# Half-row matmul units in the second output segment, 13 upper matmuls for 14, refitted bank estimate, new written orders

## The chip, the cores and the metric

One core of a Trainium2 chip runs the kernel. The metric is the device time of one execution in microseconds (us). The kernel runs in float32; its matmuls read float32r, most of them as high and low parts whose products are added up.

## The reference

The input `x` has 2048 rows of 576. Two attentions with 32 heads of width 18 are computed from it, A with keys and values of its own for each head, B with one key and one value head shared by all, and mixed by a gate:

```python
g = sigmoid((x * gate_w).sum(-1, keepdims=True))
q, k, v = split(x @ wqkv)                      # A: 32 heads of 18
a = merge(softmax(q @ k.T * 18**-0.5) @ v) @ A_wo
q, k, v = x @ B_wq, x @ B_wk, x @ B_wv         # B: k and v shared by the heads
b = merge(softmax(q @ k.T * 18**-0.5) @ v) @ B_wo
return g * a + (1 - g) * b
```

`B_wq` and `B_wk` are scaled by 8, so scores are large, and the row maximum is taken off before the exponential.

## The kernel before, in words

**Units of work.** There are 64 heads (`NU`), B's 32 first, then A's 32. A head has 16 steps (blocks of 128 keys), so there are 1024 steps, counted by `T`. A step has four banks of scores (128 keys by 512 queries each): an `s` in the written orders is one such matmul (line 674), followed by an exponential on ACT from the bank into a `pt` tile (line 682). 22 steps (`LEAD`) ahead, the maxima are made by matmuls of queries by keys (line 629): an `m` is one with a reduction on DVE (line 638); an `x` and a `y` work together, ACT taking the positive part of a difference (line 632) that DVE then joins and reduces (line 635). The sums over keys (line 689) put `pt` times values into one fixed bank, `acc`; a number in an order, 1 to 7, says how many quarters (128 columns each) of such sums follow.

**TensorE in halves.** `s` uses partitions 0 to 63 (`SB`), the maxima partitions 64 to 127 (`MB`), and the two run side by side in the two row halves of the array. The sums use all 128 rows in four column blocks. So the orders collect `s` and `m` into groups, and put the sums between the groups.

**Units.** Projections of A's values (32 units), of the later query and key rows (42), and the output projection (segments of the 1152 rows, 32 units each) are put in between. A unit is 14 (`PROJ`) or 12 matmuls into one bank of 288 to 296 columns. A whole unit, `U` (`whole_unit`, line 864), uses all 128 rows and leaves by one copy on ACT or one addition on DVE. A half unit (`half_step`, line 873) is split by rows: its upper halves, `A`, run in the half of the maxima into one bank, its lower halves, `B`, in the half of the scores into a second bank. The upper bank leaves by ACT, the lower by an addition on DVE; where the destination holds a sum already, the upper one goes through the tile `tmp`, which POOL adds. In `PROJ`'s last two entries rows 64 to 127 of the weights repeat the rows 512 to 575 of the weight matrix, and the same rows of `x` hold its low part.

**Stages.** One written order is emitted per eight steps ("a run" of it): `PLAIN` without units; `HALF14` with one half unit of 14 (steps 18 to 273 for the values, 282 to 617 for the rows); `HALF12` with one half unit of the first output segment (steps 634 to 889); `DENSE` with four whole units of the second segment (steps 946 to 1001). The last 22 steps have an order of their own and four more whole units, and the third, short segment ends the kernel.

**Banks.** Seven PSUM banks besides `acc` take everything. Which bank a matmul gets is settled when the program is written: `Clock` follows TensorE, ACT and DVE with estimated durations (lines 33 to 36), and `first` picks the bank that should be free earliest. It sets no time by itself, but a matmul whose bank is still being read waits, and TensorE runs in order.

**The rest.** `slow` is a list of generators that move on once per two steps, first in, first out: the gates, `prep_wo` (loads output weights through the tile `wost`, splits them on POOL) and `normalise` (scales a finished tile of heads on POOL). `when(T, f)` calls `f` at step `T`. All loads are issued on SP's queue in program order; POOL issues the stores of what it has made.

Of the kernel before, what the change touches and what calls it, by code (L numbers as in the profile page):

```python
# [29 lines left out]
PROJ = [(a, b, k, 128) for a, b in (("h", "h"), ("l", "h"), ("h", "l")) for k in range(NKT - 1)] + \  # L30
       [("h", "h", NKT - 1, 128), ("l", "h", NKT - 1, 128)]

PITCH_S, STREAM, HALF_MM, LOAD, GAP = 228, 214, 120, 107, 14
TO_SUMS, FROM_SUMS, QUARTER = 113, 111, 214
EXP_T, EXP_D, RED_T, RED_D, TO_ACT, TO_DVE, FREED = 477, 605, 600, 681, 459, 432, 52
COPY_T, ADD_T, MAXED, COPIED = 370, 372, 180, 400


class Unit:
    def __init__(self, ops, n, dst, done, view=lambda f: f, how="copy"):  # L40
        self.ops, self.n, self.dst, self.done, self.view, self.how = ops, n, dst, done, view, how
        self.left, self.fp = {"a": 0, "b": 0}, {}


class Clock:


    def __init__(self):
        self.free = [0.0] * 7
        self.t = self.act = self.dve = self.last = 0.0  # L50
        self.mode, self.begun, self.tail = "", [0.0, 0.0], [0.0, 0.0]
        self.turns, self.count, self.held, self.diffs = {"s": 0, "m": 0}, 0, {}, []

    def turn(self, which):
        n = self.turns[which]
# [19 lines left out]
        k = min(range(7), key=lambda i: self.free[i])  # L75
        return k, self.free[k]

    def leave(self, k, s, act, pitch, lasts):
        if act:
            at = max(s + TO_ACT, self.act)  # L80
            self.act = at + pitch
        else:
            at = max(s + TO_DVE, self.dve)
            self.dve = at + pitch
        self.free[k] = at + lasts + FREED

    def bank(self, what, tile):
        k, free = self.first()
        if what in "smxy":
            s = self.matmul(tile, free, STREAM)  # L90
            act = what in "sx"
            if what == "y" and self.diffs:
                self.dve = max(self.dve, self.diffs.pop(0))
            self.leave(k, s, act, EXP_T if act else RED_T, EXP_D if act else RED_D)
            if what == "x":
                self.diffs.append(self.free[k])
        else:
            if self.mode == "s":
                self.t = max(self.tail)
            s = max(self.t, free) + (LOAD + 14 * (HALF_MM + 11) if what != "t" else STREAM)  # L100
            self.t, self.mode = s + 99, ""
            self.leave(k, s - STREAM, what == "U", COPY_T, COPY_T + 90)
        return k

    def open(self, part, tile):
# [7 lines left out]

    def close(self, part):
        k, s = self.held.pop(part)
        self.leave(k, s + HALF_MM - STREAM, part == "a", COPY_T if part == "a" else ADD_T, 90 + ADD_T)

    def sums(self, n):
        if self.mode != "p":
            self.t += TO_SUMS if self.mode == "s" else 0  # L120
            self.mode = "p"
        self.t += QUARTER * n

    def dve_extra(self, t):
        self.dve = max(self.dve, self.t) + t


def q_row(u):
# [8 lines left out]
def gated_mix_kernel(ctx: ExitStack, tc: tile.TileContext, xT, wall, wv, wo, out):  # L137
    nc = tc.nc
    P = 128
# [361 lines left out]
    def row_units():  # L501

        pool = L["px"]
        XR, WR = [], []

        def cut(c):
            return slice(292 * c, 292 * c + 292 if c < 6 else S)

        def load_wr(mt):
            WR.append(pool.tile([P, NKT, P], F32, name="wrst"))  # L510
            load5(WR[-1], wall[mt])

        def load_xr(c):
            XR.append(pool.tile([P, 2 * NKT - 1, 296], F32R, name="xr", bufs=2))
            n = 296 if c == 6 else 292
            dma(XR[-1][:, :, 0:n], x_d[:, :, cut(c)])

        def next_w(mt):
            W = {y: pool.tile([P, NKT, P], F32R, name=f"wr{y}") for y in "hl"}
            split(WR.pop(0), W["h"], W["l"], nc.gpsimd, nc.gpsimd)  # L520
            if mt + 1 < MT:
                load_wr(mt + 1)
            return W

        def both(st, n):
            hl = pool.tile([P, 2, 296], F32R, name="rhl", bufs=1)
            split(st, hl[:, 0, 0:n], hl[:, 1, 0:n], nc.gpsimd, nc.gpsimd)
            return hl[:, :, 0:n]

        load_wr(NT)  # L530
        load_xr(0)
        W = {NT: next_w(NT)}
        yield
        for mt in range(NT, MT):
            rs = slice(mt * P, (mt + 1) * P)
            first = pool.tile([P, 4, 292], F32, name="rst", bufs=1).rearrange("p c f -> p (c f)")
            for c in range(7):
                x = XR.pop(0)
                if (mt, c) != (MT - 1, 6):
                    load_xr((c + 1) % 7)  # L540
                n = 296 if c == 6 else 292
                b = (0, 292, 584, 876, 512, 0, 808)[c]

                def done(mt=mt, c=c, n=n, b=b, first=first, rs=rs):
                    dma(qk_d[:, rs, cut(c)].rearrange("a p f -> p a f"), both(first[:, b:b + n], n), nc.gpsimd)
                    if c == 3:
                        nc.gpsimd.tensor_tensor(first[:, 0:512], first[:, 512:1024], first[:, 0:512],
                                                op=OP.subtract)
                    if 3 <= c < 5:
                        cs = slice(256 * (c - 3), 256 * (c - 2))  # L550
                        d = both(first[:, cs], 256)
                        dma(kd_d[rs, 0:2, cs], d, nc.gpsimd)
                        dma(kd_d[rs, 2, cs], d[:, 0, :], nc.gpsimd)
                    if c == 6 and mt + 1 < MT:
                        W[mt + 1] = next_w(mt + 1)

                w = W[mt]
                yield Unit([(w[a][:, k, :], x[:, k if b_ == "h" else NKT + k, 0:n]) for a, b_, k, _ in PROJ],
                           n, first[:, b:b + n], done)

    def value_units():

# [25 lines left out]
        for st_ in range(16):  # L588
            if st_ < 15:
                load(st_ + 1)  # L590
            x = XV.pop(st_)
            for hf in range(2):
                yield Unit([(x[:, k if b == "h" else NKT + k, :], w[hf][a][:, k, :]) for a, b, k, _ in PROJ],
                           288, vst[hf][:, :, 0:18],
                           lambda st_=st_, hf=hf: dma(v_d[st_, :, 304 * hf:304 * hf + 304],
                                                      vst[hf].rearrange("p h d -> p (h d)")),
                           lambda f: f.rearrange("p (h d) -> p h d", d=18))

    VG = {}

# [39 lines left out]
    def max_rows(u):  # L640


        m = ms[u % 2]
        clk.dve_extra(MAXED)
        nc.vector.tensor_reduce(m[:, 0:16], MX.pop(u), axis=AX.X, op=OP.max, negate=True)
        mt = lead.tile([P, 32], F32, name="mt")
        nc.vector.transpose(mt, m)  # L647
# [63 lines left out]
    def head_out(u):  # L711
        oe = L["work"].tile([P, 512], F32, name="oe", bufs=1)
        nc.vector.tensor_copy(oe, acc)
        clk.dve_extra(COPIED)
        sums = lambda: dma(sum_d[u].rearrange("(j f) -> j f", j=4), oe[18:128:32, :])
        if u == NU - 2:
            sums()
# [19 lines left out]
    def normalise(t, at_end=False):  # L737
# [13 lines left out]
        g = P if t >= 7 else 32  # L751
        for c in range(0, P, g):
            nc.vector.reciprocal(sm[:n, c:c + g], sm[:n, c:c + g])  # L753
            yield
        (nc.vector if at_end else nc.gpsimd).tensor_tensor(sm[:n, :], sm[:n, :], gt[:n, :], op=OP.mult)
        dma(r_d[u0:u1, :].rearrange("h (s f) -> (h s) f", f=P), sm[:n, :])
# [93 lines left out]
    def tmp_row(tag="ol", bufs=1):  # L850
        return L["work"].tile([P, 288], F32, name="tmp", tag=tag, bufs=bufs)
# [21 lines left out]
    def half_step(op):  # L873
# [8 lines left out]
            u.fp[op] = bank_tile(clk.open(op, b == MB))  # L882
        else:
            clk.more(op, b == MB)
        x, y = u.ops[n]
        nc.tensor.matmul(u.fp[op][:, 0:u.n], x[b:b + 64], y[b:b + 64], start=(n == 0), stop=(n == len(u.ops) - 1))  # L886
        u.left[op] = n + 1
        if n + 1 < len(u.ops):
            return
        HALF[op].pop(0)  # L890
        clk.close(op)
        if op == "a":
            if u.how == "copy":
                leave_unit(u, u.fp["a"], "copy")
            else:
                u.tmp = tmp_row("half", 1)
                nc.scalar.activation(u.tmp, u.fp["a"][:, 0:u.n], AF.Copy)
        else:
            leave_unit(u, u.fp["b"], "add")
# [62 lines left out]
    def when(T, f):  # L962
        at.setdefault(T, []).append(f)
# [25 lines left out]
    for t0, rows, Ta, Tb in SEG:  # L989
        when(Ta, lambda t0=t0, rows=rows: slow.append(prep_wo(t0, rows)))  # L990
        when(Tb, lambda t0=t0, rows=rows: begin_units(out_proj(t0, rows, first=t0 == 0)))
    when(950, lambda: slow.append(prep_wo(8, [P])))
    when(980, load_gates)

    def keep_busy():
# [46 lines left out]


    PLAIN = "mssmsm 4 smsmsm 3 smmssx 3 smmsys 3 mssxysm 3 msxmssm 3 mssysms 3 msssmys 4 msmsms 3 smxssm 3"
    HALF14 = "ysmssm 4 xsmsms 4 sysmms 4 sAmsAsAsm 3 msAsmBBAABsAABABmsABABmsABABmBBAxBBBx 1 smsysm 4 yssmsm 2 msms 2 msmsms 4 sxsmms 4"
    HALF12 = "mssmsx 4 mssmsm 4 smssyms 4 msmssm 4 msmssm 4 sysmms 3 mssAAmBAAsAABsAABmBsAABmBBABAxBBmBBysxs 3 smsysm 3 smsmxs 3"
    DENSE = "smsysm 4 smsmsmUsmsx 4 smsysm 4 smsmsmUsmsx 4 smsysm 4 smsmsmUsmsx 4 smsysm 4 smsmsmUsmsx 4"
    plain = [(M, c) for p in range((LEAD + 2) // 2, NSTEP // 2)
             for M, c in [(2 * p, 2), (2 * p, 3)] + [(2 * p + 1, c) for c in range(4)]]

# [131 lines left out]
```

## Time and profile before

| | us |
|---|---|
| median of 3 runs | 2680.01 (2679.63 to 2680.86) |
| profiled execution, its own time | 2681.64 |
| profiled execution, span of the instructions | 2679.9 |
| PE / DVE / ACT / POOL busy in it | 2668.6 / 2422.7 / 2413.3 / 425.0 |

The busy time of PE comes from modelled ends of pipelined matmuls, so a full PE row means that matmuls follow each other, not that the array is filled. In the rows of the trace a line of the code stands with its engine, its operation, and output and inputs; "xN" after a merged row counts instructions, and a bracket tells how long the engine was idle before it, and what ended that. Row groups give the busy time, the mean length of one in ns and the idle time before them.

### The profile page before, as it was taken

The page shows a single profiled execution, that of the slowest core. Times are in us where ns is not written, and L with a number is a line of the kernel's source. Part 1 is how long each engine was busy: PE and PEld are TensorE (multiplying, and loading weights), DVE is VectorE, ACT ScalarE, POOL GpSimd, SP SyncE. Part 2 cuts the span into 40 slices and gives each one's busy share as a digit, 9 for nine tenths or more (in the row PEclk, how much of TensorE's full clock was granted, in tenths as well). Part 3 has the DMA queues.
Part 4 walks back from the last instruction along what each step waited for, and adds up shares of the span by engine and source line. Part 5 has one row for each costly group of instructions (what it writes and reads, how often), then busy time and mean ns, then how long its engine had stood idle before and what let it go on. Part 6 is the DMA issues. An engine that isn't in the chain of part 4 may idle for free.

```text
span 2679.9 us, 61494 instructions
## 1 busy us (share of the span) xinstructions
PE 2668.6 (100%) x23032; PEld 1353.3 (51%) x23032; DVE 2422.7 (90%) x4559; ACT 2413.3 (90%) x4787; POOL 425.0 (16%) x633
## 2 busy tenths in 40 slices
PE   9999999999999999999999999999999999999998
PEld 7645454444445445454454444545454454555545
DVE  4899999999999999999999999999999999998873
ACT  4399999999999999999999999999999999998776
POOL 2810000110003212322232112000200020111002
PEclk9999999999999999999999999999999999999999
DMA  8821112321224435444455454223321332233312
GB/s 278 329 89 60 49 44 62 83 68 50 60 57 143 132 112 148 135 147 132 148 183 163 142 157 152 78 75 90 107 72 54 103 102 63 73 99 112 106 36 90
DMA packets 190127, 293.68 MB, mean 110 GB/s; under 512 B 54738, under 2 KB 149282, under 8 KB 178252
## 3 DMA queue, kind: packets, MB, share of 16 engines
q1 hardware_dynamic: 170564, 224.02, 28.7%
q0 software_dynamic: 18368, 64.50, 6.5%
q8 instruction: 181, 2.97, 0.5%
q10 hardware_dynamic: 896, 1.23, 0.1%
q14 instruction: 118, 0.97, 0.1%
HBM read 203.29 MB, written 77.62 MB: 105 GB/s over the span
## 4 chain that ended last, share of the span: by engine, by line
PE 99%; DVE 0%; DMA 0%; issue 0%; SPq 0%; ACT 0%; DVEq 0%
PE acc L689 38%; PE bank L629 26%; PE bank L674 21%; PE bank L886 7%; PE bank L255 4%; PE bank L867 3%; PE acc L701 1%; DMA wst<-wall 0%; DVE mx L638 0%; DVE oacc L862 0%; PE bank L935 0%; PE bank L302 0%; DVE rl L925 0%; SPq L143 0%; DVE sm L753 0%
## 5 line engine op out<-in xcount | busy, mean ns | idle before, releaser
L682 ACT ACTIVATE pt<-bank 128x512 f32<-128x512 f32 x4096 | 2134.7, 618 | 154.3 <-PE bank L674 72.8
L638 DVE TENSOR_REDUCE mx<-bank 128x1 f32<-128x512 f32 x3096 | 1966.4, 683 | 127.4 <-PE bank L674 60.2
L674 PE MATMUL bank<-qs,ksb 56*128 56x512 f32 x2688 | 898.6, 429 | 1.5 <-issue 1.5
L629 PE MATMUL bank<-ksb,qs 54*128 54x512 f32 x2364 | 801.5, 423 | 0.1
L674 PEld LDWEIGHTS bank<-qs,ksb 56*128 56x128 f32 x2688 | 438.2, 184 | 258.6 <-DVE mx L638 125.6
L689 PE MATMUL acc<-pt,vb 128*19 128x512 f32 (+3 forms) x5240 | 565.8, 506 | 0.0
L689 PE MATMUL acc<-pt,vg 128*19 128x512 f32 (+3 forms) x5464 | 538.4, 481 | 0.0
L629 PEld LDWEIGHTS bank<-ksb,qs 54*128 54x128 f32 x2364 | 389.4, 184 | 276.2 <-ACT pt L682 129.0
L674 PE MATMUL bank<-qs,ksa 56*128 56x512 f32 x1408 | 460.7, 433 | 0.6 <-DVE ksb L219 0.5
L629 PE MATMUL bank<-ksa,qs 54*128 54x512 f32 x1232 | 426.8, 429 | 0.0
L635 DVE CUSTOM_DVE_ANT_0 junk<-bank,xb 128x512 bf16<-128x512 f32 x500 | 342.2, 684 | 31.1 <-PE bank L629 26.0
L632 ACT ACTIVATE xb<-bank 128x512 f32<-128x512 f32 x500 | 301.3, 628 | 12.0 <-PE bank L674 11.8
L674 PEld LDWEIGHTS bank<-qs,ksa 56*128 56x128 f32 x1408 | 222.7, 184 | 151.7 <-ACT pt L682 83.6
L629 PEld LDWEIGHTS bank<-ksa,qs 54*128 54x128 f32 x1232 | 203.7, 184 | 141.9 <-ACT pt L682 82.5
L217 POOL CAST mh<-mt 128x32 fp32r<-128x32 f32 x64 | 13.5, 210 | 1389.3 <-DVE mt L647 1389.3
L689 PEld LDWEIGHTS acc<-pt,vg 128*19 128x19 f32 x5464 | 103.3, 97 | 185.2 <-issue 163.2
L689 PEld LDWEIGHTS acc<-pt,vb 128*19 128x19 f32 x5240 | 90.3, 97 | 189.3 <-issue 176.3
L629 PE MATMUL bank<-kdb,qs 54*128 54x512 f32 x372 | 150.9, 434 | 0.0
L886 PE MATMUL bank<-xr,wrh 64*128 64x292 f32 (+1 forms) x756 | 145.7, 300 | 0.0
L886 PEld LDWEIGHTS bank<-xr,wrh 64*128 64x128 f32 x756 | 124.6, 186 | 0.0
L886 PE MATMUL bank<-vwh,xv 64*128 64x288 f32 x576 | 109.5, 299 | 0.0
L217 POOL CAST rhl<-rst 128x292 fp32r<-128x292 f32 (+2 forms) x54 | 22.6, 418 | 474.2 <-DVE rst L862 436.0
(142 smaller groups left out, 1959.7 us busy)
## 6 DMA issues: line engine op xcount, KB each, us to landing
qs<-qk SPq DMA_DIRECT2D x384, 144.0 KB
xr<-x_d SPq DMA_DIRECT2D x36, 1314.0 KB
ksa<-qk SPq DMA_DIRECT2D x132, 144.0 KB
qk<-phl POOLq DMA_DIRECT2D x32, 512.0 KB, 5.8
qk<-rhl POOLq DMA_DIRECT2D x36, 292.0 KB, 3.4
ksb<-qk SPq DMA_DIRECT2D x66, 144.0 KB
xv<-x_d SPq DMA_DIRECT2D x16, 576.0 KB
onh<-oh POOLq DMA_DIRECT2D x32, 256.0 KB, 3.5
```

The costliest lines, as they stand in the source:

```text
L217: eng_h.tensor_copy(h, src)
L255: nc.tensor.matmul(fp[:, p0:p0 + g], w[a][:kr, k, :], X[b][:kr, k, x0 + p0:x0 + p0 + g], start=(n == 0), stop=(n == len(PROJ) - 1))
L629: nc.tensor.matmul(pm, qs[u % 3][b:b + 54, i * P:(i + 1) * P], k, start=True, stop=True)
L632: nc.scalar.activation(MX["x", u, i], pm, AF.Relu)
L635: nc.vector.tensor_tensor_reduce(junk, pm, MX.pop(("x", u, i)), 1.0, -3e38, op0=OP.add, op1=OP.max, accum_out=MX[u][:, i, c:c + 1])
L638: nc.vector.tensor_reduce(MX[u][:, i, c:c + 1], pm, axis=AX.X, op=OP.max)
L674: nc.tensor.matmul(ps, kst(u)[b:b + 56, i * P:(i + 1) * P], qs[u % 3][b:b + 56, c * 512:(c + 1) * 512], start=True, stop=True)
L682: nc.scalar.activation(pt, ps, AF.Exp, scale=SCALE)
L689: nc.tensor.matmul(acc[32 * j:32 * j + 19, a:b], v_of(u, i), PT[u, i, j][:, a:b], start=(i == 0), stop=(i == 15), skip_group_check=True)
L701: nc.tensor.matmul(acc[32 * j:32 * j + 19, 256 * half + a:256 * half + b], v_of(NU - 1, i), pt[:, x + a:x + b], start=(i == 0), stop=(i == ...
L867: nc.tensor.matmul(fp[:, 0:u.n], x, y, start=(n == 0), stop=(n == len(u.ops) - 1))
L886: nc.tensor.matmul(u.fp[op][:, 0:u.n], x[b:b + 64], y[b:b + 64], start=(n == 0), stop=(n == len(u.ops) - 1))
```

## The change

It does six things. The durations of `Clock` are set anew, and it follows a few more events (the copy that a DVE addition waits for, the copy of `acc` that the next sums wait for, reciprocals). A `Unit` can have fewer upper matmuls, and the value and row units have 13 for 14: the last upper one multiplies the low part of the weights by the low part of `x`, a term that is left out elsewhere too. `HALF14` and `HALF12` have other orders. `DENSE` has half units for whole ones, four per eight steps as before. The tile `tmp` of half units shares its place with `wost`. The weights of the third segment are loaded from step 908 on instead of 950.

```diff
-PITCH_S, STREAM, HALF_MM, LOAD, GAP = 228, 214, 120, 107, 14
-TO_SUMS, FROM_SUMS, QUARTER = 113, 111, 214
-EXP_T, EXP_D, RED_T, RED_D, TO_ACT, TO_DVE, FREED = 477, 605, 600, 681, 459, 432, 52
-COPY_T, ADD_T, MAXED, COPIED = 370, 372, 180, 400
+STREAM, HALF_MM, LOAD, GAP = 214, 120, 107, 18
+LEAVE, TO_SUMS, FROM_SUMS, QUARTER = 98, 15, 116, 213.4
+EXP_T, EXP_D, RED_T, RED_D, JOIN_T, TO_ACT, TO_DVE, FREED = 482, 607, 600, 682, 616, 424, 425, 52
+COPY_T, ADD_T, MAXED, COPIED = 370, 372, 430, 605
...
-    def __init__(self, ops, n, dst, done, view=lambda f: f, how="copy"):
+    def __init__(self, ops, n, dst, done, view=lambda f: f, how="copy", upper=None):
         self.ops, self.n, self.dst, self.done, self.view, self.how = ops, n, dst, done, view, how
+        self.half = {"a": ops[:upper], "b": ops}
...
     def close(self, part):
         k, s = self.held.pop(part)
-        self.leave(k, s + HALF_MM - STREAM, part == "a", COPY_T if part == "a" else ADD_T, 90 + ADD_T)
+        s += HALF_MM - STREAM
+        if part == "a":
+            end = self.on_act(s, COPY_T) + COPY_T + 55
+            self.copies.append(end + 55)
+        else:
+            self.dve = max(self.dve, self.copies.pop(0))
+            end = self.on_dve(s, ADD_T) + ADD_T + 85
+        self.free[k] = end + FREED
 
     def sums(self, n):
+        if self.mode == "s":
+            self.t = max(self.tail) + LEAVE
         if self.mode != "p":
-            self.t += TO_SUMS if self.mode == "s" else 0
+            self.t += TO_SUMS
             self.mode = "p"
-        self.t += QUARTER * n
+        self.t = max(self.t, self.cleared) + QUARTER * n
...
# row_units and value_units: the Unit gets
+                           ..., upper=-1)
...
# half_step
-        x, y = u.ops[n]
-        nc.tensor.matmul(u.fp[op][:, 0:u.n], x[b:b + 64], y[b:b + 64], start=(n == 0), stop=(n == len(u.ops) - 1))
+        last = len(u.half[op]) - 1
+        x, y = u.half[op][n]
+        nc.tensor.matmul(u.fp[op][:, 0:u.n], x[b:b + 64], y[b:b + 64], start=(n == 0), stop=(n == last))
...
-                u.tmp = tmp_row("half", 1)
+                u.tmp = L["pool"].tile([P, 288], F32, name="tmp", tag="wost")
...
-    when(950, lambda: slow.append(prep_wo(8, [P])))
+    when(908, lambda: slow.append(prep_wo(8, [P])))
...
-    HALF14 = "ysmssm 4 xsmsms 4 sysmms 4 sAmsAsAsm 3 msAsmBBAABsAABABmsABABmsABABmBBAxBBBx 1 smsysm 4 yssmsm 2 msms 2 msmsms 4 sxsmms 4"
-    HALF12 = "mssmsx 4 mssmsm 4 smssyms 4 msmssm 4 msmssm 4 sysmms 3 mssAAmBAAsAABsAABmBsAABmBBABAxBBmBBysxs 3 smsysm 3 smsmxs 3"
-    DENSE = "smsysm 4 smsmsmUsmsx 4 smsysm 4 smsmsmUsmsx 4 smsysm 4 smsmsmUsmsx 4 smsysm 4 smsmsmUsmsx 4"
+    HALF14 = "ysmssm 4 mssmsm 3 smsmsm 3 xsmssm 4 msmssm 3 msAsABABAyBsABAABAsmBABsAABmBABABmBsxmBBxs 3 smmssm 4 mssymss 4 ysxssm 4"
+    HALF12 = "msmsms 4 smmsms 2 ysms 3 smmssx 4 mssmsm 3 smsy 2 sxmsms 3 smsmsm 4 smmsAsAABBAABBmBAsABmBsAAABABByBAsxBsm 3 yssxsm 4"
+    DENSE = "msABsmBABAsAABABmBBxBAsABAABsAABmBms 4 smsmsm 5 ABAsmsABABAsyBABABABxBsAmBABsAABmB 5 msysms 7 AsmsyBBABAsAABABmBAsABmBBAAsmBABABxs 3 smsmsy 4 smABABAsmBABsAAsAmBBABmBABABBAAsmBxs 4"
```

More of the change, by code (lines that the diff above doesn't have):

```diff
@@ L51, in __init__ @@
         self.mode, self.begun, self.tail = "", [0.0, 0.0], [0.0, 0.0]
-        self.turns, self.count, self.held, self.diffs = {"s": 0, "m": 0}, 0, {}, []
+        self.turns, self.count, self.held, self.diffs, self.copies = {"s": 0, "m": 0}, 0, {}, [], []
+        self.cleared = 0.0
     def turn(self, which):
@@ L76, in first, with on_act, on_dve @@
         return k, self.free[k]
[L78 to L85, printed above, removed]
+    def on_act(self, ready, pitch):
+        at = max(ready + TO_ACT, self.act)
+        self.act = at + pitch
+        return at
+    def on_dve(self, ready, pitch):
+        at = max(ready + TO_DVE, self.dve)
+        self.dve = at + pitch
+        return at
     def bank(self, what, tile):
@@ L90, in bank @@
             s = self.matmul(tile, free, STREAM)
[L91 to L96, printed above, removed]
-        else:
-            if self.mode == "s":
-                self.t = max(self.tail)
+            if what in "sx":
+                end = self.on_act(s, EXP_T) + EXP_D
+                if what == "x":
+                    self.diffs.append(end + 60)
+            else:
+                if what == "y" and self.diffs:
+                    self.dve = max(self.dve, self.diffs.pop(0))
+                end = self.on_dve(s, RED_T if what == "m" else JOIN_T) + RED_D
+        else:
+            self.t = (max(self.tail) + LEAVE if self.mode == "s" else self.t)
             s = max(self.t, free) + (LOAD + 14 * (HALF_MM + 11) if what != "t" else STREAM)
-            self.t, self.mode = s + 99, ""
-            self.leave(k, s - STREAM, what == "U", COPY_T, COPY_T + 90)
+            self.t, self.mode = s + LEAVE, ""
+            end = (self.on_act if what == "U" else self.on_dve)(s - STREAM, COPY_T) + COPY_T + 90
+        self.free[k] = end + FREED
         return k
@@ L115, in close, with other @@
         k, s = self.held.pop(part)
-        self.leave(k, s + HALF_MM - STREAM, part == "a", COPY_T if part == "a" else ADD_T, 90 + ADD_T)
+        s += HALF_MM - STREAM
+        if part == "a":
+            end = self.on_act(s, COPY_T) + COPY_T + 55
+            self.copies.append(end + 55)
+        else:
+            self.dve = max(self.dve, self.copies.pop(0))
+            end = self.on_dve(s, ADD_T) + ADD_T + 85
+        self.free[k] = end + FREED
     def sums(self, n):
+        if self.mode == "s":
+            self.t = max(self.tail) + LEAVE
         if self.mode != "p":
-            self.t += TO_SUMS if self.mode == "s" else 0
+            self.t += TO_SUMS
             self.mode = "p"
-        self.t += QUARTER * n
-    def dve_extra(self, t):
-        self.dve = max(self.dve, self.t) + t
+        self.t = max(self.t, self.cleared) + QUARTER * n
+    def other(self, pitch, acc=False):
+        self.dve = max(self.dve, self.t) + pitch
+        if acc:
+            self.cleared = self.dve + 100
 def q_row(u):
@@ L558, in row_units @@
                 yield Unit([(w[a][:, k, :], x[:, k if b_ == "h" else NKT + k, 0:n]) for a, b_, k, _ in PROJ],
-                           n, first[:, b:b + n], done)
+                           n, first[:, b:b + n], done, upper=-1)
     def value_units():
@@ L596, in value_units @@
                                                       vst[hf].rearrange("p h d -> p (h d)")),
-                           lambda f: f.rearrange("p (h d) -> p h d", d=18))
+                           lambda f: f.rearrange("p (h d) -> p h d", d=18), upper=-1)
     VG = {}
@@ L643, in max_rows @@
         m = ms[u % 2]
-        clk.dve_extra(MAXED)
+        clk.other(MAXED)
         nc.vector.tensor_reduce(m[:, 0:16], MX.pop(u), axis=AX.X, op=OP.max, negate=True)
@@ L713, in head_out @@
         nc.vector.tensor_copy(oe, acc)
-        clk.dve_extra(COPIED)
+        clk.other(COPIED, True)
         sums = lambda: dma(sum_d[u].rearrange("(j f) -> j f", j=4), oe[18:128:32, :])
@@ L753, in normalise @@
             nc.vector.reciprocal(sm[:n, c:c + g], sm[:n, c:c + g])
+            clk.other(110 + 6.5 * g)
             yield
@@ L884, in half_step @@
             clk.more(op, b == MB)
-        x, y = u.ops[n]
-        nc.tensor.matmul(u.fp[op][:, 0:u.n], x[b:b + 64], y[b:b + 64], start=(n == 0), stop=(n == len(u.ops) - 1))
+        last = len(u.half[op]) - 1
+        x, y = u.half[op][n]
+        nc.tensor.matmul(u.fp[op][:, 0:u.n], x[b:b + 64], y[b:b + 64], start=(n == 0), stop=(n == last))
         u.left[op] = n + 1
-        if n + 1 < len(u.ops):
+        if n < last:
             return
```

## The prediction

> **What bounds the kernel now.** The order of reading: the page's busy line and chain, then the stretches by stage, then the order of time on TensorE in one group of each kind.
>
> ```profile
> span 2679.9 us, 61494 instructions
> PE 2668.6 (100%) x23032; PEld 1353.3 (51%) x23032; DVE 2422.7 (90%) x4559; ACT 2413.3 (90%) x4787; POOL 425.0 (16%) x633
> PE 99%; DVE 0%; DMA 0%; issue 0%; SPq 0%; ACT 0%; DVEq 0%
> ```
>
> The chain that ended last lies on PE for 99% of the span. DVE and ACT, which empty the PSUM banks, are busy 90%. So it is PE's own order that sets the time, and what the change takes out of that order comes off the end, unless banks then come free too late.
>
> ```profile
> core 0: us, PE busy (x) PEld busy (x) DVE busy (x) ACT busy (x) POOL busy (x), PEclk, DMA share, GB/s
> 174.09:802.49 628.40, 628.40 (x5510) 303.39 (x5506) 589.11 (x1113) 592.14 (x1185) 26.57 (x55) 1.00 0.20 59
> 821.01:1645.83 824.82, 824.82 (x7230) 400.15 (x7226) 773.67 (x1462) 777.53 (x1555) 201.73 (x303) 1.00 0.48 146
> 1682.89:2305.23 622.34, 622.34 (x5637) 310.55 (x5634) 588.49 (x1113) 594.36 (x1185) 48.42 (x81) 1.00 0.29 83
> 2305.23:2435.76 130.53, 130.43 (x1293) 65.48 (x1289) 125.13 (x237) 126.92 (x253) 22.90 (x31) 1.00 0.33 98
> 2435.76:2609.62 173.86, 173.86 (x1235) 88.72 (x1231) 141.44 (x265) 132.61 (x253) 7.68 (x13) 1.00 0.26 79
> ```
>
> These stretches begin and end at first scores matmuls of the written orders: 32 and 42 runs of HALF14, 32 of HALF12, 7 of PLAIN, 7 of DENSE. One run (eight steps) takes 628.40/32 = 19.64 us and 824.82/42 = 19.64 in HALF14, 622.34/32 = 19.45 in HALF12, 130.53/7 = 18.65 in PLAIN, 173.86/7 = 24.84 in DENSE. The granted clock is 1.00 in all of them.
>
> Now PE in DENSE, in order of time (start, length):
>
> ```profile
> 2437.65 0.50 PE L674 MATMUL bank<-qs,ksa 56*128 56x512 f32 x1
> ...
> 2437.99 0.39 PE L674 MATMUL bank<-qs,ksa 56*128 56x512 f32 x1
> ...
> 2438.22 0.39 PE L674 MATMUL bank<-qs,ksa 56*128 56x512 f32 x1
> ...
> 2438.55 0.79 PE L867 MATMUL bank<-woh,oih 128*128 128x288 f32 x4
> ...
> 2440.99 1.05 PE L689 MATMUL acc<-pt,vg 128*19 128x512 f32 x8
> 2441.98 0.50 PE L674 MATMUL bank<-qs,ksa 56*128 56x512 f32 x1
> ...
> 2442.88 1.05 PE L689 MATMUL acc<-pt,vg 128*19 128x512 f32 x8
> 2443.87 0.50 PE L674 MATMUL bank<-qs,ksa 56*128 56x512 f32 x1
> ```
>
> A plain group (three scores and three maxima in the two row halves, then four quarters of sums) goes from 2441.98 to 2443.87: 0.90 to the sums, 0.99 for them. A pair costs 0.23 (2437.99 to 2438.22; in the sums below 0.228, the 214 + 14 ns of the kernel's own constants). The group with a whole unit goes from 2437.65 to 2441.98, 4.33 us; five pairs without a unit would take 0.90 + 2 x 0.23 + 0.99 = 2.35. So a whole unit costs 1.98 us, though 12 matmuls at the 0.134 of the next rows make 1.61: the rest lies around them, from 2438.22 to the first of the unit at 2438.55 and behind the last.
>
> The same for HALF14's long group, and HALF12's:
>
> ```profile
> 1024.91 0.49 PE L629 MATMUL bank<-ksb,qs 54*128 54x512 f32 x1
> ...
> 1025.49 0.30 PE L886 MATMUL bank<-xr,wrh 64*128 64x292 f32 x1
> 1025.62 0.30 PE L886 MATMUL bank<-xr,wrl 64*128 64x292 f32 x1
> ...
> 1025.76 0.29 PE L886 MATMUL bank<-xr,wrl 64*128 64x292 f32 x1
> ...
> 1028.23 0.41 PE L689 MATMUL acc<-pt,vb 128*19 128x128 f32 x8
> 1028.58 0.50 PE L674 MATMUL bank<-qs,ksb 56*128 56x512 f32 x1
> ```
>
> ```profile
> 2005.46 0.50 PE L629 MATMUL bank<-ksb,qs 54*128 54x512 f32 x1
> ...
> 2009.37 0.85 PE L689 MATMUL acc<-pt,vg 128*19 128x128 f32 x16
> ```
>
> A half matmul takes 0.134 of its row half (0.27 for two, 1025.49 to 1025.76). One quarter of sums takes 0.35 (1028.23 to 1028.58) and four 0.99, so n quarters take 0.13 + 0.214n, and a group's fixed part is 0.13 there and 0.90 - 3 x 0.23 = 0.21 before its sums: 0.34 in all.
>
> With these prices I add up each order: in each group a matmul starts when its row half is done with the one before it (0.228 or 0.134 later) and not ahead of the one before it in the order. HALF14's long group comes to 3.32 by that sum and took 1028.23 - 1024.91 = 3.32. A whole run of HALF14 now comes to 19.49 (took 19.64, so 0.14 of waits for banks), HALF12 to 19.10 (19.45, 0.35), PLAIN to 17.98 (18.65, 0.67), DENSE to 24.81 (24.84, 0.03). HALF12's long group alone took 3.91 for a sum of 3.72.
>
> **The change, part by part.**
>
> *Half units in DENSE.* Out go four whole units, 4 x 1.98 = 7.92 us per run; in come 48 matmuls in each row half, 48 x 0.134 = 6.43, balanced in every group. The order has 7 groups for 8: -0.34. By the sum of the groups a run is 22.94 for 24.81, -1.87. What leaves the banks becomes more: ACT copies each unit's upper half, and POOL adds it.
>
> ```profile
> L856 ACT ACTIVATE oacc<-bank 128x288 f32<-128x288 f32 x32 | 14.6, 455 | 0.0
> L219 POOL TENSOR_TENSOR rhl<-rst,rhl 128x292 fp32r<-128x292 f32 (+2 forms) x54 | 43.0, 797 | 4.4
> 2496.39 0.67 POOL L217 CAST woh<-wost 128x576 fp32r<-128x576 f32 x1 [30.64 <-DMA wost<-wo]
> 1023.55 4.54 ACT L682 ACTIVATE pt<-bank 128x512 f32<-128x512 f32 x9 [0.23 <-PE bank L674]
> 1014.60 3.06 DVE L638 TENSOR_REDUCE mx<-bank 128x1 f32<-128x512 f32 x5
> ```
>
> ACT was busy 132.61/173.86 = 76% there; four copies of at most 0.455 make 20.8 us of 23, 90%. That is below HALF14's 592.14/628.40 = 94%, where waits come to 0.14, so I take 0.10 of waits (ends 0.03, as today, and 0.3) and 23.04 per run: -1.80 x 7 = **-12.6 us** (ends -12.9 and -11.2). The one buffer for the copied half is a new wait: the next copy on ACT stands behind POOL's add, and all exponentials queue behind that copy. The closest two upper halves end 4.17 us apart by the same sum; the add needs the lower half's end 0.23 later, DVE's add and 0.8 on POOL, about 2 us in all. If one of POOL's normalisation pieces (two operations) gets in between, cover is still left; were it gone, it would cost a microsecond or two in the first two runs only. The earlier loading of the last weights counts here: today POOL stood 30.64 us for their DMA in the middle of DENSE, harmless then; in front of the adds it would have stopped ACT. Moved to step 908, its two DMAs on SP, the cast and the subtraction on POOL lie in PLAIN, ahead of the last normalisation (step 916); the loads of queries and keys that they pass on SP are for heads two and more later, and nothing needs the weights before the end: 0.
>
> *HALF14, 74 runs.* Nine groups for ten (-0.34), one upper matmul less per unit; but the row halves differ in two groups by a full matmul. The sum: seven plain groups 6.25, "mssymss" 1.12, the long group 3.82 (its order has 15 banks and 13 + 14 half matmuls), sums 32 x 0.214 + 9 x 0.13 = 8.01; together 19.20 for 19.49, -0.30. The thirteenth upper matmul dropped only helps the balance: the lower half still has 14. Waits are the open term. Lower end: what each group gives ACT and DVE to do, at 0.49 per exponential (4.54 for nine, the last 0.62 long) and 0.60 per maximum. The long group has nine on ACT, 9 x 0.49 + 0.37 = 4.78 for a length of 4.59; HALF12's long group of today has ten, 5.27 for 4.49, and lost 0.19. The groups with three quarters give DVE 1.80 for 1.66, never more than two in a row. That makes 0.10. (0.37 is the kernel's constant for a copy; the row has 0.455, of which a part overlaps the next.) Upper end: waits against ACT's share over the stages are 0.14 at 94.2%, 0.35 at 95.5%, 0.67 at 97.2%; HALF14's 18.50 us of ACT per run in about 19.5 makes 95%, 0.3. I take 0.19, nearer to the lower end because today's two groups with only two quarters in HALF14, which give DVE up to 1.80 for 1.45, are gone: 19.39, -0.25 x 74 = **-18.6 us** (ends -25.2 at 0.10, -8.3 at 0.33).
>
> *HALF12, 32 runs.* Ten groups for nine, long group balanced (7 and 7): the sum is 19.21 for 19.10, worse by 0.11. It pays only if the waits of 0.35 fall: the long group now gives ACT 8 x 0.49 + 0.37 = 4.29 for 4.26. I take 0.20, 19.41: **-1.2 us** (ends -4.5 at 0.10, +3.5 at 0.35).
>
> *The refitted estimate* moves no work; it changes which of seven banks each result goes to. In PLAIN, whose order stays, that is all there is: 12 runs by 0.1 either way, 0 (ends -1.2 and +1.2). The last 22 steps keep their order: 0.
>
> Sum: -12.6 - 18.6 - 1.2 = -32.4. The profiled execution took 2681.6 for a span of 2679.9; the median of the runs is 2680.0, so the span moves to 2647.5 and the median to **2647.6**.
>
> **A rule weighed.** HALF14's long group holds two banks for its unit, as the new DENSE does, and lost nothing by it: 3.32 for a sum of 3.32. The Trainium skill, "TensorEngine Tiling (Array Packing)", Gotcha 1 (PSUM Pressure), speaks against the change: row tiling raises the pressure on PSUM, since different row tiles must write to different banks. By the row DENSE keeps its -12.6; by the rule the outcome would be the first rival's.
>
> **Rivals.**
>
> *Two banks held.* If the half units' banks cost 0.19 in every long group (HALF12's excess today), DENSE with its four loses 0.76 and keeps 1.14 x 7 = 8.0, HALF14 waits 0.14 + 0.19 = 0.33, and HALF12 0.35 as now: -8.0 - 8.3 + 3.5 = -12.8, 2667. For it: fifteen banks in HALF14's long group, as in HALF12's today. Against it: the 3.32.
>
> *Slower: the new picks send work to banks that come free late.* All of the smaller sums of HALF14 and HALF12 would turn into waits on banks. With w of waits per run in both, the change is 74 (w - 0.44) + 32 (w - 0.24) - 12 us, so it is slower from w = 0.49 on. At PLAIN's 0.67: +17 + 14 - 8.6 (DENSE too) = +22, 2702. For it: PLAIN shows that 0.67 happens at ACT 97%, DVE 96%. Against it: HALF14 would be at 94%.
>
> *The picks are right to the last.* Waits near 0.05 everywhere: -29.0 - 6.0 - 13, 2632.
>
> **How the numbers follow.** The forecast (2636 to 2665: -25.2 - 4.5 - 12.9 - 1.2 and -8.3 + 3.5 - 11.2 + 1.2) gets 0.67; still faster 0.06; two banks held (2665 to 2674) 0.12; no change 0.05; slower 0.10. A change of 0.2%, 5.4 us, is what a measurement here can tell. Faster 0.67 + 0.06 + 0.12 = 0.85, same 0.05, slower 0.10. The range 2634 to 2668 leaves out about 0.2.
>
> **What would show it.** DENSE runs of 23.0 us (right) or above 23.6 (banks or POOL's buffer); ACT copies waiting for POOL would name the buffer. HALF14 at 19.4 per run with nine groups; a long group far over 3.82 names the banks. HALF12 at 19.4, its long group at 3.5. PLAIN at 18.6 shows the estimate neutral. I am wrong if HALF14 stays at 19.6, since it carries more than half of the sum.

## The result: 2657.3 us for 2680.3, and the profile after

The changed kernel takes 2657.27 us (median of 4 runs, 2656.58 to 2658.60) where the kernel before takes 2680.26: a ratio of 0.9915, 95% interval 0.9898 to 0.9932, 23.0 us less. The forecast was 2647.6 in a range of 2634 to 2668.

The page of the changed kernel; its lines are 16 to 18 higher than before: 674, 629, 689, 886 are now 690, 645, 705, 904:

```profile
span 2654.8 us, 66482 instructions
PE 2644.7 (100%) x25414; PEld 1412.0 (53%) x25414; DVE 2413.2 (91%) x4559; ACT 2430.4 (92%) x4815; POOL 447.9 (17%) x661
PE 99%; DMA 0%; DVE 0%; ACT 0%; issue 0%; ACTq 0%; DVEq 0%
```

TensorE still sets the end. ACT has 28 more instructions, the copies of DENSE's upper halves, and POOL 28 more, their additions. By stages (columns as before; the two stretches of HALF14, then HALF12 and DENSE, from first scores matmul to first scores matmul):

```profile
173.38:795.50 622.12, 622.12 (x5989) 316.89 (x5985) 586.59 (x1113) 595.02 (x1185) 26.58 (x55) 1.00 0.20 59
814.04:1631.40 817.36, 817.36 (x7860) 416.79 (x7856) 770.72 (x1463) 781.98 (x1555) 202.00 (x303) 1.00 0.49 147
1668.49:2293.00 624.51, 624.51 (x6405) 324.25 (x6401) 587.52 (x1113) 596.55 (x1185) 48.45 (x81) 1.00 0.28 83
2422.96:2584.51 161.55, 161.55 (x1739) 103.90 (x1735) 138.97 (x264) 140.05 (x281) 30.07 (x42) 1.00 0.28 86
```

| stage | before, us per run | after | change in all | forecast |
|---|---|---|---|---|
| HALF14, 74 runs | 19.64 | 19.45 | -13.7 | -18.6 |
| HALF12, 32 runs | 19.45 | 19.52 | +2.2 | -1.2 |
| DENSE, 7 runs | 24.84 | 23.08 | -12.3 | -12.6 |
| all else | | | -1.3 | 0 |

These make 25.1, the difference of the two spans. It is 2.1 more than the difference of the medians, because the profiled execution before lies 1.4 above its median (2681.64 for 2680.26) and the one after 0.7 below (2656.58 for 2657.27).

### The profile page after: what moved, and what is told of

It reads as the page before. It is cut to its first block, busy times and chain, and to the rows that moved or that the text cites. A ratio compares the mean times of both kernels' runs of the same rounds, so it can differ in the third digit from the quotient of the medians.

```text
span 2654.8 us, 66482 instructions
## 1 busy us (share of the span) xinstructions
PE 2644.7 (100%) x25414; PEld 1412.0 (53%) x25414; DVE 2413.2 (91%) x4559; ACT 2430.4 (92%) x4815; POOL 447.9 (17%) x661
## 4 chain that ended last, share of the span: by engine, by line
PE 99%; DMA 0%; DVE 0%; ACT 0%; issue 0%; ACTq 0%; DVEq 0%
PE acc L705 38%; PE bank L645 27%; PE bank L690 20%; PE bank L904 8%; PE bank L271 4%; PE bank L884 1%; PE acc L717 1%; DMA xsh<-xT 0%; DVE mx L654 0%; DMA wst<-wall 0%; DVE oacc L879 0%; PE bank L953 0%; PE bank L318 0%; ACT xh L360 0%; DVE xl L366 0%; PE bank L939 0%
## 5 line engine op out<-in xcount | busy, mean ns | idle before, releaser
L654 DVE TENSOR_REDUCE mx<-bank 128x1 f32<-128x512 f32 x3096 | 1943.8, 684 | 112.2 <-PE bank L645 51.5
L645 PE MATMUL bank<-ksb,qs 54*128 54x512 f32 x2364 | 822.0, 428 | 0.1
L705 PE MATMUL acc<-pt,vb 128*19 128x512 f32 (+3 forms) x6216 | 554.6, 452 | 0.0
L705 PE MATMUL acc<-pt,vg 128*19 128x256 f32 (+3 forms) x6608 | 541.6, 427 | 0.0
L645 PE MATMUL bank<-ksa,qs 54*128 54x512 f32 x1232 | 442.1, 431 | 0.0
L705 PEld LDWEIGHTS acc<-pt,vg 128*19 128x19 f32 x6608 | 139.4, 97 | 232.2 <-issue 194.9
L705 PEld LDWEIGHTS acc<-pt,vb 128*19 128x19 f32 x6216 | 124.4, 97 | 197.6 <-issue 161.6
L904 PE MATMUL bank<-xr,wrh 64*128 64x292 f32 (+1 forms) x756 | 111.8, 300 | 0.0
L904 PEld LDWEIGHTS bank<-xr,wrh 64*128 64x128 f32 x756 | 92.9, 186 | 1.9
L904 PE MATMUL bank<-vwh,xv 64*128 64x288 f32 x576 | 84.6, 298 | 0.0
```

The lines of the kernel that those rows point to most:

```text
L645: nc.tensor.matmul(pm, qs[u % 3][b:b + 54, i * P:(i + 1) * P], k, start=True, stop=True)
L654: nc.vector.tensor_reduce(MX[u][:, i, c:c + 1], pm, axis=AX.X, op=OP.max)
L705: nc.tensor.matmul(acc[32 * j:32 * j + 19, a:b], v_of(u, i), PT[u, i, j][:, a:b], start=(i == 0), stop=(i == 15), skip_group_check=True)
```

## The experiments

The question was where HALF14 and HALF12 lost what their sums had promised, and which part of the change brings what. "Per run" is a stage's stretch by its number of runs, for HALF14 both stretches by 74. "Excess" is what a group takes from its first matmul to its sums over the prediction's sum, a mean over the runs of a stage (of HALF14's two stretches the second, where only one is named), from the starts of the matmuls in the order of time. A group is named by its letters; the long group is the one with the half unit. A group's "banks" are its s, m, x and y, beside the two that the unit holds. Medians come from three or five rounds of timing beside the kernel before.

**DENSE alone, and the estimate alone.** In the kernel before, first only DENSE is changed (with `tmp`'s place and step 908):

```diff
-                u.tmp = tmp_row("half", 1)
+                u.tmp = L["pool"].tile([P, 288], F32, name="tmp", tag="wost")
-    when(950, lambda: slow.append(prep_wo(8, [P])))
+    when(908, lambda: slow.append(prep_wo(8, [P])))
-    DENSE = "smsysm 4 smsmsmUsmsx 4 ..."
+    DENSE = "msABsmBABAsAABABmBBxBAsABAABsAABmBms 4 ..."
```

> The kernel before with half units in DENSE alone (the new DENSE order, tmp in the place of wost, the last weights at step 908; old estimate, old HALF14 and HALF12, 14 upper matmuls). Theory: DENSE is worth its own share whatever else is changed: 23.1 us per run for 24.84, so -12.3 us in all, about 2668, with HALF14 and HALF12 as before (19.64, 19.45). Rival: the old estimate places the half units' two banks badly, and DENSE is at 23.5 or more, -9 us or less.

Then only the estimate (the class `Clock`, its durations and its calls):

> The kernel before with the new estimate alone (its durations and what it follows); all orders and units as before. Theory: the picks of banks hardly matter, since the waits come from the work that ACT and DVE have in a group: within 3 us of before, waits per run of HALF14 0.14 and HALF12 0.35 as before. Rival: the estimate carries the gain: HALF14 and HALF12 lose half of their waits, 0.07 and 0.17 per run, -11 us.

The stretches, the second of HALF14 and DENSE with DENSE alone, then HALF14's two with the estimate alone:

```profile
819.61:1644.30 824.69, 824.69 (x7230) 400.24 (x7226) 774.01 (x1462) 777.44 (x1555) 202.05 (x303) 1.00 0.48 146
2434.30:2595.97 161.67, 161.67 (x1741) 103.95 (x1737) 139.15 (x264) 139.88 (x281) 30.11 (x42) 1.00 0.28 87
```

```profile
173.77:800.65 626.88, 626.84 (x5510) 300.64 (x5506) 588.03 (x1113) 592.32 (x1185) 26.61 (x55) 1.00 0.20 59
819.18:1641.63 822.45, 822.40 (x7230) 395.69 (x7226) 772.69 (x1462) 777.79 (x1555) 202.10 (x303) 1.00 0.48 146
```

DENSE alone: 2668.33, ratio 0.9957 (0.9940 to 0.9973), 161.67/7 = 23.10 per run with HALF14 where it was. That is what was expected: the half units are worth 12.2 us by themselves, with the old estimate as with the new one (12.3). The estimate alone: 2676.25, ratio 0.9984 (0.9975 to 0.9994), HALF14 at 19.59 for 19.64; of its groups one moved, "msms", from 0.07 or 0.08 of excess to 0.01. Here neither the theory (within 3 us) nor the rival (11 us less) held: the picks matter, but only at single places.

**The old estimate in the changed kernel.**

> The changed kernel with the old estimate: new orders, 13 upper matmuls, half units in DENSE. Theory (picks hardly matter): within 3 us of the changed kernel's 2657, HALF14 at 19.45 per run. Rival (the new orders need the new estimate): waits per run in HALF14 rise from 0.26 to 0.4 or more, +10 us or more, 2667 or more.

```profile
173.31:798.40 625.09, 625.09 (x5988) 315.46 (x5985) 587.32 (x1113) 594.67 (x1185) 26.58 (x55) 1.00 0.20 58
816.93:1637.60 820.67, 820.67 (x7859) 413.87 (x7856) 771.56 (x1463) 780.54 (x1555) 201.98 (x303) 1.00 0.49 146
```

2663.77, ratio 0.9939 (0.9924 to 0.9954), 6.5 above the changed kernel and so between the two expectations; HALF14 at 19.54. Two groups carry it: "smsmsm" 0.12 of excess for 0.06, the long group 0.15 for 0.11. So of HALF14's 13.7 us the orders and the 13 matmuls bring 7.5, the refit 6.3.

**Fourteen upper matmuls, late and early.** Both kernels drop `upper=-1` from the changed kernel and add one A to HALF14's long group; the sum of the groups is the same.

```diff
-    ... msAsABABAyBsABAABAsmBABsAABmBABABmBsxmBBxs 3 ...
+    ... msAsABABAyBsABAABAsmBABsAABmBABABmABsxmBBxs 3 ...     # late
+    ... msAsABABAAyBsABAABAsmBABsAABmBABABmBsxmBBxs 3 ...     # early
```

> The changed kernel with all 14 upper matmuls in the value and row units, so one more A in HALF14's long group (behind the group's last but two lower ones, ahead of the last scores but one). Theory: the upper row half is the longer one in the new long group (8 full and 13 half matmuls against 7 and 14), so the fourteenth adds its 0.134 to every run: 19.58 for 19.45, +10 us, 2667. Rival: the long group waits for ACT and its banks anyway, and the matmul hides in that: +3 us or less.

> The changed kernel with all 14 upper matmuls, as in the first run with fourteen, but with the added A early in the unit (in front of the y) instead of after the others; the sum of the groups is the same, 19.33 per run. Theory (a unit's bank is lost to the stream for as long as the unit is open, and the late A held it longer): the excess of the long group is back at 0.10 to 0.12, HALF14 at 19.59, +10 on the changed kernel, 2667, where the late A made +25. Rival (a matmul more in the upper half costs that, wherever it stands): 19.80, +25, 2682.

Late, then early:

```profile
175.55:808.39 632.84, 632.84 (x6022) 325.14 (x6018) 586.62 (x1113) 598.07 (x1185) 26.61 (x55) 1.00 0.20 58
826.91:1659.43 832.52, 832.52 (x7901) 427.68 (x7897) 770.61 (x1463) 785.17 (x1555) 202.25 (x303) 1.00 0.48 144
```

```profile
173.54:799.27 625.73, 625.73 (x6021) 320.18 (x6017) 587.62 (x1113) 597.46 (x1185) 26.55 (x55) 1.00 0.20 58
817.78:1640.32 822.54, 822.54 (x7902) 421.82 (x7898) 771.57 (x1463) 785.68 (x1555) 201.90 (x303) 1.00 0.48 146
```

Late: 2682.66, ratio 1.0009 (1.0000 to 1.0019), HALF14 at 19.80, +0.35 per run for one matmul of 0.134, more than either expectation; the long group's excess rises from 0.11 to 0.34 in the second stretch. Early: 2665.34, ratio 0.9942 (0.9929 to 0.9956), 19.57, +0.12, excess 0.10, about as without it. Same instructions, same sum, 17 us apart. The waits in one long group with the late A name what it costs beyond itself (who waited for whom; us in total, times, longest; L873 is the copy of the unit's upper half):

```profile
ACT rst L873 <- PE bank L904: 0.3, 1, 0.3
PEld bank L690 <- ACT rst L873: 0.2, 1, 0.2
```

ACT stands until the late A is done, and the group's last score waits for the copy that empties the unit's bank. Over the second stretch these two waits come once in each of the 42 runs (11.4 and 8.7 us); with the A early, and in the changed kernel, neither comes at all.

**What makes the long group's excess.** First the work: ACT's share in it is lowered, its 15 banks are kept.

```diff
-    ... msAsABABAyBsABAABAsmBABsAABmBABABmBsxmBBxs 3 smmssm 4 mssymss 4 ...
+    ... msAsABABAyBsABAABAsmBABsAABmBABABmBsxmBBms 3 smmssm 4 xssymss 4 ...
```

> The changed kernel with one exchange in HALF14: the last x of the long group becomes an m, and the first m of the group 'mssymss' becomes an x. The sum of the groups stays at 19.20 and the long group keeps its 15 banks, but gives ACT eight exponentials and a copy for nine, and DVE seven maxima and an addition for six. Theory (ACT's work makes the 0.10 that the long group takes over its sum): the excess falls to 0.03, HALF14 at 19.38, 2652. Rival (fifteen banks through the five that the unit leaves make it): the excess stays at 0.10, HALF14 at 19.45, 2657.

Then the time for which the unit's two banks are held: the same matmuls, spread over the group (the order that it replaces is the changed kernel's, above).

```diff
+    ... msAsAByBABAsmBABAsmBABAsxBABAsmBABABmsABxB 3 smmssm 4 mssymss 4 ...
```

> The changed kernel with the same matmuls in HALF14's long group (15 banks, 13 upper and 14 lower), but spread evenly, so that the unit's two banks are held from the start of the group to its end; the row halves come free in step, and the sum of the groups is 0.04 less, 19.16. Theory (holding time of the two banks): the long group's excess is 0.4 or more, HALF14 at 19.8 or more, +26 on the changed kernel, 2683. Rival (ACT's and DVE's work in the group, which is the same): 19.41, -3, 2654.

The exchange, the spread order, and the spread long group in the order of time on TensorE:

```profile
821.87:1649.76 827.89, 826.81 (x7860) 423.32 (x7856) 769.42 (x1463) 781.92 (x1555) 202.03 (x303) 1.00 0.48 145
```

```profile
826.71:1659.40 832.69, 832.69 (x7860) 425.46 (x7856) 771.84 (x1463) 789.40 (x1555) 201.76 (x303) 1.00 0.48 144
```

```profile
1132.99 0.50 PE L645 MATMUL bank<-ksb,qs 54*128 54x512 f32 x1
...
1137.18 0.52 PE L705 MATMUL acc<-pt,vb 128*19 128x384 f32 x4
```

and the changed kernel's own long group:

```profile
1017.46 0.50 PE L645 MATMUL bank<-ksb,qs 54*128 54x512 f32 x1
...
1021.37 0.84 PE L705 MATMUL acc<-pt,vb 128*19 128x384 f32 x8
```

The exchange left the long group's excess at 0.12, with less work for ACT; what it cost (2674.73, ratio 0.9977, 0.9967 to 0.9987; 19.70 per run) lies in the group that got the x, 0.19 of excess for 0.02, and in "mssmsm", 0.06 for 0.00. It is a weak test of ACT's work, though: the exchanged matmul is the last but one of the group, and the matmuls ahead of it start as late in one kernel as in the other. It shows only that this one exponential does not make the excess, and it gave DVE a maximum in its place.

The spread order takes 1137.18 - 1132.99 = 4.19 for a sum of 3.78, where the changed kernel takes 1021.37 - 1017.46 = 3.91 for 3.82: on average 0.42 of excess against 0.11, with the same number of exponentials, maxima and copies and the same 15 banks. The group behind, "smmssm", loses another 0.11. 2683.84, ratio 1.0012 (1.0003 to 1.0021). So the amount of work does not make the difference. Between the unit's first and last A stand 7 of the 15 banks in the changed order, 12 in the spread one. The closing time alone is not it: 0.23 of the excess has arisen by the second plain maximum behind the y, 1.5 us into the group, where the changed kernel, with its unit open as well, has lost 0.01 (both beyond the 0.11 by which every group's second matmul in a row half comes late). This points to what is asked for while the unit holds two banks. The spread order also moves the s, m, x and y among themselves, and no run separates that.

**Level orders.** Groups made level by moving an x from the long group to the group with four scores, which then has eight banks; the long group in the order in which the row halves come free.

```diff
-    HALF14 = "... msAsABABAyBsABAABAsmBABsAABmBABABmBsxmBBxs 3 smmssm 4 mssymss 4 ysxssm 4"
+    HALF14 = "... msAsABmBABAsmBABAsyBABAsmBABAsmBABABxsABB 3 smmssm 4 msxsysms 4 ysxssm 4"
-    HALF12 = "msmsms 4 smmsms 2 ysms 3 ..."
+    HALF12 = "mssmsx 4 mssmsm 4 smsysxms 4 msmssm 4 msmssm 4 sysmms 3 msABAsmBABAsmBABAsyBABAsmBABAsmBABAsxB 3 smsysm 3 smsmxs 3"
```

> The changed kernel with another HALF14: an x moves from the long group to the group with four scores, so that all groups are level (7 and 7, 4 and 4), and the long group's matmuls stand in the order in which their row halves come free. The sum of the groups is 19.06 for 19.20, with 14 banks in the long group for 15. Theory (the sum sets the time, the waits per run stay at 0.26): 19.32, -9.6, 2648. With the long group's excess gone: 19.24, -16, 2642. Rival (ACT and DVE take back what PE gains, waits grow with ACT's share): 19.42, -3 or less, 2655.

> The changed kernel with another HALF12: nine groups as in the kernel before, but level, with one x moved to the group with four scores and the long group in the order in which the row halves come free. The sum is 18.79 for 19.21. Theory (the sum sets the time, waits per run 0.30 as now): 19.10, -13, 2644. Rival (ACT and DVE take it back: ACT would be busy 97%, as in PLAIN with its 0.58): 19.37, -5, 2653.

> The changed kernel with both level orders (HALF14 and HALF12). Both theories: the stages are far apart and the gains add: the sum of what the two orders bring alone, -23 by the sums with today's waits, -8 if ACT and DVE take it back.

HALF14's second stretch with its level order, HALF12's with its own, and the group of eight in HALF14 (PEld is the weight load, whose bracket names what it waited for):

```profile
833.40:1675.88 842.48, 841.63 (x7859) 428.33 (x7855) 760.85 (x1462) 797.34 (x1555) 201.98 (x303) 1.00 0.47 143
```

```profile
1669.37:2304.83 635.46, 635.46 (x5638) 312.78 (x5634) 584.43 (x1113) 604.54 (x1185) 48.46 (x81) 1.00 0.28 82
```

```profile
1149.93 0.49 PE L645 MATMUL bank<-ksb,qs 54*128 54x512 f32 x1
...
1150.51 0.39 PE L690 MATMUL bank<-qs,ksb 56*128 56x512 f32 x1
...
1150.80 0.18 PEld L645 LDWEIGHTS bank<-ksb,qs 54*128 54x128 f32 x1 [0.34 <-DVE mx L654]
...
1151.15 0.18 PEld L690 LDWEIGHTS bank<-qs,ksb 56*128 56x128 f32 x1 [0.16 <-ACT pt L698]
...
1151.58 0.14 PEld L705 LDWEIGHTS acc<-pt,vb 128*19 128x19 f32 x8 [0.24 <-issue]
```

HALF14 level: 2701.88, ratio 1.0077 (1.0062 to 1.0092), 20.05 per run for 19.45. HALF12 level: 2668.26, ratio 0.9951 (0.9936 to 0.9966), 19.86 for 19.52. Both: 2712.17, ratio 1.0116 (1.0099 to 1.0133): the losses add (44.6 + 11.0; 54.9 measured). All three had been expected to be faster than the changed kernel; all three are slower. The rows show why: six banks are filled by 1150.51, the seventh matmul starts at 1150.80 behind a maximum on DVE, the eighth at 1151.15 behind an exponential, and 1.65 us pass for a sum of 1.12. A group of eight without a unit has an excess of 0.52 in HALF14 and 0.49 in HALF12, one of six or seven 0.00 to 0.15, and 0.19 where it begins with an x ("xssymss" above). The long groups, whose units stay open nearly throughout, have 0.30 and 0.42.

**Another estimate, and a HALF12 sought with it.** Three durations are changed, meant to come nearer to the stages measured so far; how near they come, no run here shows.

```diff
-EXP_T, ..., TO_ACT, TO_DVE, FREED = 482, 607, 600, 682, 616, 424, 425, 52
+EXP_T, ..., TO_ACT, TO_DVE, FREED = 490, 607, 600, 682, 616, 480, 480, 52
+    HALF12 = "smmsms 4 mssmsm 3 mssmsm 3 xssyms 4 mssmsm 4 smmxssm 3 smABAsAmBBAsAAByBsAABmBsAAABABsmBBxBsy 3 ysmsssm 4 mssmxs 4"
```

> The changed kernel with another HALF12 of nine groups (none above seven banks beside the long one, the unit open for a short time) and an estimate with 0.490 per exponential for 0.482 and 0.480 to the start on ACT and DVE for 0.424. Theory: HALF12 at 19.40 for 19.52, -3.6, and HALF14 a little lower by better picks, 19.42, -2: together 2651 to 2654, faster than both kernels. Rival (the picks are as good as they get, ACT takes back what the order saves): 2657, the same as the changed kernel.

```profile
816.60:1637.30 820.70, 820.70 (x7860) 414.32 (x7856) 771.31 (x1463) 780.40 (x1555) 201.47 (x303) 1.00 0.49 146
1674.38:2298.68 624.30, 624.30 (x6149) 326.87 (x6146) 592.46 (x1114) 594.71 (x1185) 48.33 (x81) 1.00 0.28 83
```

2662.61, ratio 0.9933 (0.9920 to 0.9947). HALF14 is at 19.54 with the very excesses of the old estimate (0.12 in "smsmsm", 0.15 in the long group), HALF12 at 19.51, no gain; both expectations were lower (2651 to 2654, and 2657). Which durations make those two groups' picks good was not settled.

**The old HALF12 in the changed kernel.**

> The changed kernel with the HALF12 of the kernel before; all else as changed. Theory (the new HALF12 is a small loss: its sum is 0.11 higher and its waits fall by only 0.04 per run): HALF12 back at 19.44 for 19.52, -2.3, 2655, the fastest of all. Rival (the new order gains by what it does to the stage's neighbours or to the picks): 2657 or more.

```profile
1669.57:2291.88 622.31, 622.31 (x5637) 307.72 (x5634) 588.56 (x1113) 594.51 (x1185) 48.44 (x81) 1.00 0.28 83
```

2655.23, ratio 0.9905 (0.9888 to 0.9921), HALF12 at 622.31/32 = 19.45 for 19.52, as expected. It is the lowest of all medians; the 2 us to the changed kernel are below what the times can tell, but the stage shows them.

## Why the prediction held, and which terms were off

**The bound and the sums of the groups held.** Every group beside the long ones comes within some hundredths of its sum in HALF14, HALF12 and DENSE of the changed kernel; the largest excess is that of "smsmsm" (0.06 in HALF14, 0.08 in HALF12). PLAIN, which the change leaves as it was, keeps 0.59 per run over a sum of 17.98.

**DENSE: right in mechanism and size.** 23.08 per run for a forecast of 23.04. The four groups that hold a unit have excesses of 0.02 to 0.04, not the first rival's 0.19. The new wait behind POOL did not come: the additions take 0.81, and ACT in DENSE waited for TensorE alone (the first row gives durations in ns, least, median and largest, and the first and last start; the others are waits as above):

```profile
L919 POOL TENSOR_TENSOR oacc<-tmp,oacc x28: 797/808/817, 2427.3 to 2584.7; 128x288 f32<-128x288 f32 x28
```

```profile
ACT pt L698 <- PE bank L690: 15.7, 24, 0.9
ACT pt L698 <- PE bank L645: 3.2, 10, 0.6
ACT tmp L915 <- PE bank L690: 1.3, 6, 0.2
ACT tmp L915 <- PE bank L904: 0.2, 1, 0.2
```

That late weights would have stopped ACT is argued only; no run loads them late. (One slip in the sum: waits of 0.03 make -13.1 for DENSE, not -12.9; nothing hangs on it.)

**HALF14: the term for waits was too small.** It is 0.26 per run, forecast 0.19, inside its ends (0.10 to 0.33); that is 4.9 of the 7.3 us by which the span missed its forecast (HALF12 has 3.4 and DENSE 0.3 of them, the rest gave 1.3 back). The step that failed is the lower end, to which the 0.19 leaned: it was drawn from ACT's and DVE's work per group and gave 0.10 for the whole run. The long group alone has that, 0.09 and 0.11 in the two stretches. The other 0.15 lie mostly where the prediction saw no wait: 0.06 in "smsmsm", the second of two groups with three quarters in a row, 0.03 in "xsmssm", 0.02 in "mssymss". With the old estimate "smsmsm" has 0.12, so the picks bear on it.

That the long group's share matches the lower end does not show the lower end's reason. With the work unchanged its excess went from 0.10 with the early A to 0.34 with the late one, and from 0.11 to 0.42 with the spread order. The first rival, two banks held, had this mechanism, at 0.19 where the changed kernel has 0.11. The upper end, a line through three stages by ACT's share, came nearer by luck: the spread order waits 0.66 per run at a share of 789.40/832.69 = 94.8%, the level one 0.99 at 797.34/842.48 = 94.6%, both below the 95.7% of the changed kernel.

**HALF12: the same term, and the sign.** Its sum rose by the forecast 0.11, its waits fell from 0.35 to 0.30 only, not to 0.20. The long group keeps 0.17 of excess (0.19 before), though ACT has eight exponentials and not ten. Nor does the open time alone order the groups: by the sum this unit is open for 2.20 us in each half, HALF14's for 2.29 and 2.79 with less excess. What does separate them in all runs is how many banks the group asks for beside the unit's: with at most 12 (DENSE, and HALF14's long group before) the excess is 0.05 or less, with 14 or 15 it is 0.07 to 0.42, though no run changes that number alone. Why HALF12's is 0.17 stays open.

**The fourteenth upper matmul: a step that was wrong.** I wrote that dropping it "only helps the balance: the lower half still has 14". In the new long group the upper half has eight full matmuls and is the longer one, so the matmul is worth 0.12 per run, 9 us, where it stands early, and 0.35, 26 us, where it keeps the unit open until the last score needs its bank. The total did not suffer, since the order was summed with 13.

**The estimate: put at nothing, worth 4 to 6 us.** PLAIN, the only place I looked, hardly moved (18.57 for 18.65 in its last stretch); HALF14 did, in the kernel before by one group, in the changed kernel by two.

The rival on the slow side, waits from 0.49 on, has its mechanism: the level orders reached 0.99 in HALF14 (20.05 for a sum of 19.06) by groups that ask for more banks than there are. The written orders of the change avoid this: no group without a unit has more than seven banks. The rule weighed (the Trainium skill, "TensorEngine Tiling (Array Packing)", Gotcha 1, row tiling raises the pressure on PSUM) agrees with HALF14's rows, where the long group's excess is 0.10 to 0.42 with 14 or 15 banks beside the two held ones, and hardly shows in DENSE's 0.02 to 0.04 with 10 to 12.

## What to carry to other kernels

Where one engine's written order bounds a kernel, add the order up group by group from the trace's own steps, and test the sum on the kernel you have, before believing it for another order: the sums were good to hundredths, and nearly all that went wrong was in the waits. Count an accumulator not only as work but as a bank that is gone while it is open: see what else is asked for in that time, close it early, and let no burst ask for more banks than exist. Judge an estimate that settles an order by the places where it changes a pick: here one or two groups carried all that it was worth.

## What was not expected of the hardware

One half-row matmul of 0.134 us cost 0.35 per run where the last score had to wait for its bank, and 0.12 where it stood earlier. With seven banks beside that of the sums, six or seven filled in one burst cost 0.00 to 0.19 of excess, eight 0.49 to 0.52: the last two matmuls wait until a maximum and an exponential have emptied a bank.
